# Moving seven stores behind the value loads, and the second feature pair's loads a tile forward, between two gates of a gMLP

## The chip, the cores and the metric

The kernel runs on one core of one Trainium2 chip. The metric is the device time of one execution in microseconds (us). Before the change it was 1759.82 us in the median of three runs (1759.15 to 1762.06). Executions of the same program differ by some 3 us, so a change of 2 us can hardly be read from whole times.

In the traces, PE is the matmul engine (TensorE), DVE is VectorE, ACT is ScalarE, and SP is the engine that issues all DMAs here, in one queue and in the order of the program.

## The reference, cut to what matters

The reference is an attention block followed by a gated MLP. The change sits in the second half:

```python
z  = gelu(einsum('bsd,df->bsf', h, w_in))          # h: 2048 tokens x 1024
z1 = z[..., :1792]
z2 = layernorm(z[..., 1792:], axis=-1)              # the "values"
g  = einsum('ts,bsf->btf', w_sp, z2) + b_sp[None, :, None]    # the "gate": mixes tokens
y  = einsum('bsf,fd->bsd', z1 * g, w_out)           # the "projection"
x  = x + gb * y
```

## The kernel before

The kernel makes the gate for tokens 0 to 1023 (the first gate), projects four token tiles of that half, makes the gate for tokens 1024 to 2047 (the second gate), and projects the rest. The features are cut into seven pairs of 256 (`p` = 0 to 6). One block of a gate handles one pair: it makes four output quarters with seven products of eight 128x128 by 128x512 matmuls. Some operands are sums or differences of quarters, which VectorE makes (`z_sum`). The values wait in DRAM; each pair is loaded in two loads (`k` = 0 and 1, 512 KB each, one for each half of the tokens that are summed over), and ScalarE norms them in place, eight 128x256 operations for each load.

```python
def load_z(c, p, k):                    # value load, L1408
    t = zr[c, p, k] = heap.take("zr", [P, 8, 256], FP16)
    nc.sync.dma_start(t[:], z2_dram[8 * k:8 * k + 8, :, p * 256:(p + 1) * 256]
                      .rearrange("t p f -> p t f"))

def norm_z(c, p, k, ts=range(8), by_dve=False):
    for t in ts:                        # ScalarE, L1418
        z, q = zr[c, p, k][:, t, :], 8 * k + t
        # ... (a branch for VectorE is cut)
        nc.scalar.activation(z, z, ACT.Identity, scale=z_rs[:, q:q + 1], bias=z_nm[:, q:q + 1])

def z_sum(c, p, m):                     # VectorE; m == 1 is L1429, and needs both loads' values
    a11, a21, a12, a22 = (zq(c, p, k, i) for k in range(2) for i in range(2))
    if m == 1:
        zs[c, p] = heap.take("zs", [P, 2, 8, P], FP16)
        nc.vector.tensor_add(out=zs[c, p][:, 0], in0=a21, in1=a22)
    # ... (m = 2, 3, 4 are cut)

def store_zk():                         # gated features of tokens 512..1023, kept for the end; L1617
    for p in range(NG):
        nc.sync.dma_start(zk_dram[p], z1T[0, p][:, :, 512:1024])

def project(ti, between=()):            # one token tile of the projection
    if ti + 2 < 4:
        load_x1(ti + 2)                 # residual of a later tile, L1559
    # ... 28 matmuls into bo (L1569), outt = bo + residual on VectorE (L1490),
    # ... some of VectorE's waiting tasks, then the output store (L1577)
```

The hooks of a gate block fix VectorE's order. The ones that matter:

```python
g.on(1 if p else 2, lambda: norm_z(c, p + 1, 0))
g.on(7, lambda: z_sum(c, p + 1, 1))
g.on(5, lambda: z_sum(c, p + 1, 3), lambda: z_sum(c, p + 1, 2))
g.on(5, lambda: norm_z(c, p + 2, 1))
```

And the loop that the change edits:

```python
for ti in range(4):
    if ti == 1:
        load_z(1, 0, 0)
        load_z(1, 0, 1)
        store_zk()
    elif ti == 2:
        load_b(1)                       # the bias, L1403
        load_z(1, 1, 0)
        load_z(1, 1, 1)
        load_z(1, 2, 1)
        norm_z(1, 0, 0)
        norm_z(1, 0, 1)
    project(ti, last + [weights] if not ti else ())
while tasks:
    tasks.pop(0)()
heap.give(*(z1T[0, p] for p in range(NG)))
norm_z(1, 1, 1)
```

The softmax here doesn't subtract the row's maximum and nothing guards it: scores larger than these inputs give would overflow.

## Time and profile before

| what | value | view |
|---|---|---|
| time | 1759.82 us (1759.15 to 1762.06, 3 runs) | the runs |
| span of the profiled run | 1760.4 us, granted clock 1.0 | the page |
| PE busy | 1740.1 us, 99% | the page, part 1 |
| matmul to matmul, 512 columns | 0.216 us | timeline of PE |
| PE's delays in the first 25 us of the second gate | 0.61 + 1.60 = 2.21 us | timeline of PE |
| ScalarE starts the second pair's norms | 1.83 us after the gate's first matmul | timeline of ACT |

Lines of the page, before:

```profile
span 1760.4 us, 23835 instructions
...
PE 1740.1 (99%) x8542; PEld 799.5 (45%) x8542; DVE 1502.9 (85%) x2284; ACT 1298.5 (74%) x1529; POOL 30.5 (2%) x39
...
PE 88%; DVE 6%; DMA 3%; ACT 2%; issue 1%; SPq 0%; DVEq 0%; ACTq 0%
```

PE is busy nearly all the time. The Trainium skill ("Perfetto Trace Analysis", Identifying the Most-Contended Engine) warns that matmul busy time is a bad measure of the distance to the roofline, because matmuls are pipelined. Here, too, busy time hides what matters: one matmul's record lasts 0.379 us but the next starts 0.216 us later, so a delay is seen best in the distance from start to start. 0.216 us is what the skill gives for a warm array ("TensorE: Matmul & The Clock Gate", Wait — 56ns, not 53.3ns?: 215.7 ns for 512 columns), and this trace agrees. I call *delay* what a distance has over 0.216 us.

From the timeline of PE, before: start, duration, engine, line, operation and tiles, count, and in brackets the idle time before and what ended it. The first line is the start of the second gate.

```profile
1606.66 1.03 PE L965 MATMUL a<-s_slots,zr 128*128 128x512 f16 x4
...
1617.90 1.03 PE L965 MATMUL c<-s_slots,zr 128*128 128x512 f16 x4
1619.38 1.89 PE L965 MATMUL a<-h_slots 128*128 128x512 f16 x8 [0.45 <-DVE snap L1490]
1622.70 1.02 PE L965 MATMUL a<-wq_t 128*128 128x512 f16 x4 [1.44 <-DVE snap L1490]
```

Four matmuls from 1617.90 should end their turn at 1618.77; the next starts at 1619.38. Eight from 1619.38 should end theirs at 1621.11; the next starts at 1622.70. Both times PE waited for a snapshot that VectorE takes of a PSUM bank before PE may go on accumulating in it. The reader should not stop there. The chain of waits, before (start, duration, what), leads further back:

```profile
1599.86 8.54 DMA zr<-z_dram
...
1608.49 2.12 ACT zr L1418 x5
...
1610.96 5.51 ACT zr L1418 x11
...
1616.49 0.69 DVE wq_t L1429
1617.18 1.20 DVE w_t_15636 L1390 x2
1618.39 0.33 DVE units L1612
1618.72 0.61 DVE snap L1490
...
1622.04 0.61 DVE snap L1490
...
1622.70 1.89 PE a L965 x8
```

A value load of 8.54 us from its issue to its landing, then sixteen norms, then the sum that needs them, and behind that sum, in VectorE's order, the snapshots. The timelines of ACT and DVE, before, show the idle time at both hand-overs:

```profile
1598.36 4.03 ACT L1418 ACTIVATE h_slots<-h_slots,z_nm,z_rs 128x256 f16<-128x256 f16 x8
1608.49 11.90 ACT L1418 ACTIVATE zr<-zr,z_nm,z_rs 128x256 f16<-128x256 f16 x24 [6.10 <-DMA zr<-z_dram]
...
1614.12 0.41 DVE L1612 TENSOR_TENSOR w_out<-w_out 128x512 f16<-128x512 f16 x1
1616.49 0.69 DVE L1429 TENSOR_TENSOR wq_t<-zr 128x1024 f16<-128x1024 f16 x1 [1.96 <-ACT zr L1418]
```

And the DMA queue, before, shows why the load came late: stores are issued first (and, not shown here, a residual, an output store and the bias).

```profile
1590.32 0.70 SPq L1408 DMA_DIRECT2D h_slots<-z_dram  x1
1591.06 3.71 SPq L1617 DMA_DIRECT2D zk_dram<-z1T  x4
...
1599.27 5.64 SPq L1408 DMA_DIRECT2D zr<-z_dram  x3
```

### The profile page before, as it was taken

What the parts mean: (1) busy time and instruction counts of PE and PEld (TensorE: products, weight loads), DVE (VectorE), ACT (ScalarE), POOL (GpSimd) and SP (SyncE); (2) the same over time, 40 slices, a digit from 0 to 9 for tenths busy, and PEclk for the clock granted to TensorE, in tenths of its full rate; (3) what the DMA queues carried; (4) which work ended last, traced back from release to release, by engine and by line L of the source; (5) the groups of instructions that cost most, each with busy time, mean ns of one, the idle gap of its engine ahead of it and who ended that gap; (6) DMA issues with size and microseconds to landing.
All of it is one profiled execution on the core that took longest, in us unless ns stands there. A gap on an engine that the chain in (4) does not pass through costs nothing.

```text
span 1760.4 us, 23835 instructions
## 1 busy us (share of the span) xinstructions
PE 1740.1 (99%) x8542; PEld 799.5 (45%) x8542; DVE 1502.9 (85%) x2284; ACT 1298.5 (74%) x1529; POOL 30.5 (2%) x39
## 2 busy tenths in 40 slices
PE   7999999999999999999999999999999999999999
PEld 4444444444444444444444444444444444444444
DVE  6898898898988898989999988986679788788975
ACT  6998889999999999999999999711235666736600
POOL 1000000000000000000000000000000000000000
PEclk9999999999999999999999999999999999999999
DMA  8575466646544643555653474645758544558222
GB/s 252 132 181 143 114 142 160 160 126 151 156 131 130 165 114 96 145 138 137 160 123 102 116 189 127 189 125 159 177 154 218 143 122 122 179 128 219 61 78 96
DMA packets 452999, 253.52 MB, mean 144 GB/s; under 512 B 293776, under 2 KB 412816, under 8 KB 452880
## 3 DMA queue, kind: packets, MB, share of 16 engines
q1 hardware_dynamic: 452880, 252.00, 54.2%
q8 instruction: 67, 1.10, 0.3%
q14 instruction: 52, 0.43, 0.1%
HBM read 146.02 MB, written 55.59 MB: 115 GB/s over the span
## 4 chain that ended last, share of the span: by engine, by line
PE 88%; DVE 6%; DMA 3%; ACT 2%; issue 1%; SPq 0%; DVEq 0%; ACTq 0%
PE sps L509 23%; PE ops L777 23%; PE a L965 16%; PE b L965 9%; PE c L965 4%; PE qa L490 4%; PE qps L407 4%; PE qb L490 3%; DMA wm<-in_w_mod_dram 1%; ACT pt L840 1%; PE bo L1569 1%; PE a_11218 L965 1%; PE mps L201 1%; DVE sum L1013 0%; DMA zr<-z_dram 0%
## 5 line engine op out<-in xcount | busy, mean ns | idle before, releaser
L840 ACT ACTIVATE pt<-sps 128x1024 bf16<-128x1024 f32 x1008 | 1004.6, 1024 | 80.9 <-PE sps L509 37.3
L509 PE MATMUL sps<-qT,kT 128*128 128x512 bf16 x2048 | 609.2, 379 | 2.4 <-ACT pt L840 1.2
L777 PE MATMUL ops<-pt,v_sb 128*128 128x512 bf16 x2048 | 598.9, 379 | 0.0
L509 PEld LDWEIGHTS <-kT 128*128 128x128 bf16 x2048 | 199.3, 98 | 246.5 <-issue 14.8
L777 PEld LDWEIGHTS <-v_sb 128*128 128x128 bf16 x2048 | 200.1, 98 | 243.2 <-issue 1.6
L1008 ACT ACTIVATE snap<-a 128x512 f32<-128x512 f32 (+1 forms) x111 | 60.7, 565 | 115.4 <-PE a L965 105.0
L965 PEld LDWEIGHTS <-h_slots 128*128 128x128 f16 (+1 forms) x716 | 70.0, 98 | 84.1 <-issue 1.6
L856 DVE COPY ou<-ops 128x512 f32<-128x512 f32 x126 | 81.1, 686 | 30.0 <-PE ops L777 27.4
L407 PE MATMUL qps<-h1T,wq_t 128*128 128x512 bf16 x288 | 96.7, 379 | 0.0
L1013 DVE TENSOR_TENSOR sum<-b,snap 128x512 f32<-128x512 f32 (+1 forms) x76 | 50.0, 658 | 46.9 <-PE b L965 28.0
L1418 ACT ACTIVATE zr<-zr,z_nm,z_rs 128x256 f16<-128x256 f16 x90 | 45.0, 586 | 47.9 <-DMA zr<-z_dram 40.9
L665 DVE TENSOR_TENSOR oT<-ou,rbc 128x1024 bf16<-128x1024 f32 x62 | 75.3, 1214 | 1.4 <-DMA rbc<-rec_dram 1.4
L475 DVE COPY tx<-qa 128x512 f32<-128x512 f32 x66 | 45.4, 688 | 31.3 <-PE qa L490 31.3
L643 DVE TENSOR_REDUCE den<-pT 128x8 f32<-128x1024 bf16 x58 | 68.7, 1185 | 0.7 <-DMA pT<-sums_dram 0.7
L965 PEld LDWEIGHTS <-s_slots 128*128 128x128 f16 (+1 forms) x415 | 40.3, 98 | 50.5 <-DVE s_slots L1338 1.5
L490 PE MATMUL qa<-h1s,wq_t 128*128 128x512 f16 x176 | 63.0, 379 | 0.0
L490 PEld LDWEIGHTS <-wq_t 128*128 128x128 bf16 (+1 forms) x352 | 34.4, 98 | 41.6
L965 PEld LDWEIGHTS <-wq_t 128*128 128x128 f16 (+1 forms) x344 | 33.6, 98 | 40.8 <-DVE wq_t L1431 1.0
L148 POOL TENSOR_TENSOR rstd<-var,neg_half 128x1 f32<-128x1 f32 x30 | 25.0, 835 | 1303.1 <-DVE var L146 1275.4
L470 DVE TENSOR_TENSOR qT<-qb,tx 128x512 bf16<-128x512 f32 x66 | 45.2, 684 | 0.7
L407 PEld LDWEIGHTS <-wq_t 128*128 128x128 bf16 x288 | 28.2, 98 | 33.9 <-issue 0.6
L490 PEld LDWEIGHTS <-tx 128*128 128x128 f16 x264 | 25.8, 98 | 31.2
(962 smaller groups left out, 2575.0 us busy)
## 6 DMA issues: line engine op xcount, KB each, us to landing
rbc<-rec_dram SPq DMA_DIRECT2D x63, 512.0 KB
v_sb<-in_A_v_cache_dram SPq DMA_DIRECT2D x40, 512.0 KB
oT_dram<-oT SPq DMA_DIRECT2D x62, 256.0 KB
sums_dram<-pacc SPq DMA_DIRECT2D x58, 256.0 KB
wm<-in_w_mod_dram SPq DMA_DIRECT2D x12, 1024.0 KB
wq_t<-in_A_wq_dram SPq DMA_DIRECT2D x7, 1024.0 KB
zr<-z_dram SPq DMA_DIRECT2D x12, 512.0 KB
h_slots<-oT_dram SPq DMA_DIRECT2D x10, 512.0 KB
```

The source lines that it names most:

```text
L407: nc.tensor.matmul(box["ps"][:], weights[:, dc, hc:hc + DH], src[:, dc, q0:q0 + 512], start=(n == 0), stop=(n == KD - 1))
L475: nc.vector.tensor_copy(out=x if m == 6 else su, in_=a)
L490: nc.tensor.matmul(box["b" if m in (2, 7, 4) else "a"][:], *operand(m, dc), start=(m in (1, 2, 7) and dc == 0), stop=(dc == 3), skip_group ...
L509: nc.tensor.matmul(sps[:, j * 512:(j + 1) * 512], kts[h][:, kb * P:(kb + 1) * P], qts[(h, qh)][:, j * 512:(j + 1) * 512], start=True, stop ...
L643: nc.vector.tensor_reduce(out=den[:], in_=state[i]["pT"][:], op=ALU.add, axis=mybir.AxisListType.X)
L665: nc.vector.tensor_mul(out=oT, in0=state[i]["ou"][:], in1=state[i]["rbc"][:])
L777: nc.tensor.matmul(o_ps[j][:], vs[halves[i][0]][:, kb, :], pt_tiles[g][:, j * 512:(j + 1) * 512], start=(kb == 0), stop=(kb == NKB - 1))
L840: nc.scalar.activation(pt_tiles[g], s_tiles.pop(g)[:], ACT.Exp, scale=SCALE, **bias)
L856: nc.vector.tensor_copy(out=ou[:, j * 512:(j + 1) * 512], in_=o_ps[j][:])
L965: nc.tensor.matmul(self.ps[self.BANK[n]], a, b, start=(n in (1, 2, 7) and k == 0), stop=(k == len(lhs) - 1), skip_group_check=True)
L1008: nc.scalar.activation(t, ps, ACT.Copy)
L1013: nc.vector.tensor_add(out=t, in0=ps, in1=snap)
```

## The change

The seven stores are not needed until the end of the kernel; the second pair's values are needed within 10 us. The change moves the stores behind the value loads and loads the second pair right behind the first pair, one projection tile sooner. It also writes the norms sooner in the program and swaps the two loads of each pair, so that the one normed first is loaded first.

```diff
     for ti in range(4):
         if ti == 1:
-            load_z(1, 0, 0)
-            load_z(1, 0, 1)
+            for k in ((0, 1), (0, 0), (1, 1), (1, 0)):
+                load_z(1, *k)
+        elif ti == 2:
+            norm_z(1, 0, 1)
+            norm_z(1, 0, 0)
+            load_b(1)
             store_zk()
-        elif ti == 2:
-            load_b(1)
-            load_z(1, 1, 0)
-            load_z(1, 1, 1)
             load_z(1, 2, 1)
-            norm_z(1, 0, 0)
-            norm_z(1, 0, 1)
+        elif ti == 3:
+            norm_z(1, 1, 1)
         project(ti, last + [weights] if not ti else ())
     while tasks:
         tasks.pop(0)()
     heap.give(*(z1T[0, p] for p in range(NG)))
-    norm_z(1, 1, 1)
```

## The prediction

> **What bounds the kernel now.** TensorE. The page gives PE 1740.1 us busy of a 1760.4 us span (99%), granted clock 1.0, and the chain that ended last is 88% PE. The change touches the stage between first and second gate: the four projection tiles of the first half (1585 to 1607 us) and the first two blocks of the second gate (1607 to 1625 us). In PE's timeline, 512-column matmuls follow each other every 0.216 us there; from 1480 us to the end only three places are later: 0.61 us before 1619.38, 1.60 us before 1622.70, 0.29 us before 1691.8. So at most 2.2 us, 0.13% of the span, is to be had.
>
> **Where those 2.2 us come from.** The waits put both on VectorE's snapshots (L1490). The chain of waits goes further back: snapshot <- value sum (L1429) <- ScalarE norms (L1418) <- a value load. In the DMA queue, the second pair's loads are issued at 1599.3 and 1599.9 us, after seven stores of gated features (1591.1 to 1597.2), a residual load, an output store and the bias; by their semaphores they land at 1606.6 and 1608.4. ScalarE, idle for 6.1 us, starts norming at 1608.49; two tiles of 8 x 0.5 us end at 1616.49; VectorE sits idle 1.96 us before the sum that needs them. The Trainium skill ("DMA: Bandwidth & Descriptors", Issuing engines are not separate DMA queues) says all DMAs run on the same 16 engines and interleave; in this trace landings follow the order of issue, about 0.65 us per 256 KB store and 1.6 us per 512 KB load.
>
> **What the change does.** No arithmetic and no bytes are added or removed; some buffers change. The second pair's loads move from behind the stores to right behind the first pair's: issued at about 1591 and 1592, landed at about 1597.7 and 1599.4. ScalarE then norms four tiles without a break, 1594.4 to about 1610.5, six us sooner. The stores go out about 1596.5 to 1602.5 and land by about 1609; VectorE's first unit, which rewrites a stored buffer, comes at 1612: 3 us to spare. The buffers that the early loads take were last read by PE before 1585.1 us, so they should not block the queue. The third pair's load lands about 1 us later, before ScalarE wants it.
>
> **How much is critical.** VectorE's idle 1.96 us goes. Its order stays, so I step its durations on from 1614.46: sum 0.61, two weight sums 1.21, unit 0.33, snapshot to 1617.3 (PE wants it at 1618.8: first gap gone), then gate, product, two value sums, unit, snapshot to about 1620.6, against PE's 1620.5. The second gap shrinks to 0.1-0.3 us. Gain 2.0 us. Thereafter VectorE is as far behind PE as now, without a stall: nothing is given back. Predicted 1757.8 us, range 1756.2 to 1759.6; the spread of runs (1759.15 to 1762.06) is as large as the gain. Faster by over 2%: 0.005; within 2%: 0.99; slower: 0.005.
>
> **What would show it.** Right: value loads landed by 1600; ScalarE's 6.1 us idle and VectorE's wait for the norms gone; PE's two gaps together under 0.4 us; all later work 2 us earlier, the gap near 1690 unchanged. Wrong: units or later value loads wait for the late stores (a new gap at 1612 to 1640); the early loads delay the residual load of tile 3 or the queue blocks on the output store; or they slow the first pair so that the first gate product starts late.

## The result

After: 1759.23 us in the median of four runs (1757.53 to 1760.77); before, in the same rounds and with the earlier runs, 1760.17 us (1759.15 to 1762.06). The ratio is 0.9993 with a 95% interval of 0.9976 to 1.001: no change within 2%, and nothing that these runs can tell from noise.

Lines of the page, after:

```profile
span 1755.8 us, 23842 instructions
...
PE 1737.0 (99%) x8542; PEld 797.9 (45%) x8542; DVE 1502.9 (86%) x2284; ACT 1298.6 (74%) x1529; POOL 30.5 (2%) x39
...
PE 92%; DVE 5%; DMA 1%; ACT 1%; issue 1%; SPq 0%; DVEq 0%; ACTq 0%
```

The profiled spans differ by 4.6 us, but not all of that is the change. The second gate's first matmul starts at 1606.66 us before and at 1604.08 us after, but the projection's first matmul is already 2.58 us sooner (1576.45 against 1579.03 us), and PE had no delay in the projection of either run: these 2.58 us lie ahead of anything that the change could touch. The rest, 2.04 us, lies in the stage. From the timeline of PE, after:

```profile
1604.08 1.03 PE L965 MATMUL a<-s_slots,h_slots 128*128 128x512 f16 x4
...
1615.32 1.03 PE L965 MATMUL c<-s_slots,zr 128*128 128x512 f16 x4
1616.18 1.89 PE L965 MATMUL a<-h_slots,zr 128*128 128x512 f16 x8
1618.07 1.02 PE L965 MATMUL a<-wq_t 128*128 128x512 f16 x4
```

The first delay is gone (1615.32 to 1616.18 is four matmuls' time), and of the second 0.165 us is left (1616.18 to 1618.07, where eight matmuls take 1.73). The timelines of ACT and DVE, after:

```profile
1591.60 4.04 ACT L1418 ACTIVATE zr<-zr,z_nm,z_rs 128x256 f16<-128x256 f16 x8 [30.42 <-DMA zr<-z_dram]
1595.54 4.02 ACT L1418 ACTIVATE h_slots<-h_slots,z_nm,z_rs 128x256 f16<-128x256 f16 x8
1599.47 11.89 ACT L1418 ACTIVATE zr<-zr,z_nm,z_rs 128x256 f16<-128x256 f16 x24
...
1611.54 0.41 DVE L1612 TENSOR_TENSOR w_out<-w_out 128x512 f16<-128x512 f16 x1
1611.88 0.68 DVE L1429 TENSOR_TENSOR wq_t<-zr 128x1024 f16<-128x1024 f16 x1
```

ScalarE's 6.10 us of idle time and VectorE's 1.96 us are gone. The DMA queue, after, has all four loads ahead of the stores:

```profile
1588.49 2.85 SPq L1408 DMA_DIRECT2D zr<-z_dram  x2
...
1594.42 2.66 SPq L1617 DMA_DIRECT2D zk_dram<-z1T  x4
```

To compare the two runs, I give landings in us from the second gate's first matmul. They are the last of each DMA's sixteen semaphore increments in the trace.

```
                        before    after
first pair, loads   -12.33 -10.63   -12.57 -10.43
second pair, loads   -0.02  +1.74    -8.62  -6.88
seven stores         -9.95..-5.71    -4.14..-0.12
tile 3's residual       -5.08    -6.09
bias                    -1.92    -4.82
third pair, load        +3.38    +1.54
```

### The profile page after: what moved, and what is told of

The parts are those of the page before. It is cut to its first block, busy times and chain, and to the rows that moved or that the text cites. A ratio compares the mean times of both kernels' runs of the same rounds, so it can differ in the third digit from the quotient of the medians.

```text
span 1755.8 us, 23842 instructions
## 1 busy us (share of the span) xinstructions
PE 1737.0 (99%) x8542; PEld 797.9 (45%) x8542; DVE 1502.9 (86%) x2284; ACT 1298.6 (74%) x1529; POOL 30.5 (2%) x39
## 4 chain that ended last, share of the span: by engine, by line
PE 92%; DVE 5%; DMA 1%; ACT 1%; issue 1%; SPq 0%; DVEq 0%; ACTq 0%
PE sps L509 24%; PE ops L777 24%; PE a L965 16%; PE b L965 9%; PE c L965 4%; PE qa L490 4%; PE qps L407 4%; PE qb L490 3%; PE bo L1569 1%; ACT pt L840 1%; DMA wm<-in_w_mod_dram 1%; PE a_11218 L965 1%; PE mps L201 1%; DVE sum L1013 0%; DVE stats L154 0%
```

## The experiments

Eleven more runs were made (e1 is the changed kernel again), all with correct results; all profiled runs had a granted clock of 0.998 to 1.0. Runs with a profile alone: I compare only stage times, never their whole times. For each I read the same numbers, in us: when the second pair's last norm ends and when its sum starts on VectorE, both from the second gate's first matmul; PE's delays within 25 us of that matmul (one of 0.02 us that nearly all profiles have is left out); and the *stage time*, from the second gate's first matmul to the end of the kernel's last one.

| kernel | norms end | sum starts | PE's delays | stage time |
|---|---|---|---|---|
| before | +9.80 | +9.83 | 2.21 | 150.76 |
| after | +3.35 | +7.80 | 0.17 | 148.72 |
| after again (e1) | +3.73 | +7.80 | 0.17 | 148.73 |
| order of norms and first pair alone (e6) | +9.44 | +9.47 | 1.85 | 150.41 |
| two loads swapped alone (e3) | +8.17 | +8.20 | 0.59 | 149.15 |
| stores moved alone (e2) | +6.06 | +7.80 | 0.17 | 148.73 |
| loads moved alone (e4) | +3.26 | +8.26 | 0.65 | 149.19 |
| loads moved, residual ahead (e11) | +4.07 | +7.80 | 0.17 | 148.73 |
| loads later still (e5) | +11.20 | +11.23 | 3.60 | 152.17 |
| after, stores last (e9) | +3.52 | +7.80 | 0.17 | 148.72 |
| after, one VectorE move (e7) | +3.54 | +7.80 | 0.00 | 148.57 |
| after, two VectorE moves (e8) | +3.47 | +7.80 | 0.00 | 148.44 |
| e8, products 3 and 4 swapped (e10) | +3.54 | +7.80 | 0.00 | 148.40 |

Before was profiled only once. But in every profile the stage time less all of PE's delays (the one near the end of the gate included, 0.29 us in most) is 148.25 to 148.29 us, although e1 to e11 ran on three different chips. So, to within 0.04 us, the stages differ by PE's delays and by nothing else.

My theory is that only one time counts, the end of the second pair's norms; VectorE reaches the sum at +7.80 by itself, and every microsecond that the norms end later is a microsecond of PE. The rivals are that the stores must leave the way because they compete for the DMA engines, that the sooner place in the program counts, and that part of the gain is given back later.

### e1: the changed kernel again, five rounds

No edit.

> The changed kernel again, five rounds. Theory (only PE's two gaps in the first blocks of the second gate go): mean 2 us under before, ratio about 0.9988; the profile shows 0.17 us left of the 2.21 us of gaps there. Rival (the medians, 0.94 us apart, are right and half of the gain is given back somewhere): ratio about 0.9995, and a new gap after 1640 us. Either ratio may be within the noise; the gaps decide.

Measured: 1758.70 us in the median (1757.19 to 1759.24), against 1760.77 us (1758.31 to 1761.85, nine runs) of before on the same chip; ratio 0.9989, interval 0.9976 to 1.0001. The profile shows 0.17 us of delay in the stage and the old 0.29 us near the end of the gate, nothing new. The mean lies where the theory has it, but the interval just includes no change; the stage time, 148.73 against 148.72 us, is what repeats. Nothing is given back.

### e6: the program's order alone

```diff
         if ti == 1:
-            load_z(1, 0, 0)
             load_z(1, 0, 1)
+            load_z(1, 0, 0)
             store_zk()
         elif ti == 2:
+            norm_z(1, 0, 1)
+            norm_z(1, 0, 0)
             load_b(1)
             load_z(1, 1, 0)
             load_z(1, 1, 1)
             load_z(1, 2, 1)
-            norm_z(1, 0, 0)
-            norm_z(1, 0, 1)
+        elif ti == 3:
+            norm_z(1, 1, 1)
```

(and the `norm_z(1, 1, 1)` behind the loop taken away)

> Before, with only the order in the program changed as the change has it: the first pair's two loads swapped, its norms written ahead of the bias and the loads, the second pair's first norm written a projection tile sooner. Loads of the second pair and stores stay. Theory: ScalarE has nothing else to do there and waits for data, so nothing moves: gaps 2.2 us. Rival (norming sooner in the program helps): gaps under 1.5 us.

Measured: 1.85 us of delay, so most of it stays, as the theory had it, but not exactly 2.21. The 0.36 us of difference is the same 0.36 us by which the norms ended sooner (9.44 against 9.80): the second pair's later load happened to land that much sooner against PE in this run (+1.39 against +1.74). ScalarE was idle until its data came, wherever the norms stood in the program. This part of the change does nothing for the time by itself.

### e3: the second pair's two loads swapped, nothing else

```diff
             load_b(1)
-            load_z(1, 1, 0)
             load_z(1, 1, 1)
+            load_z(1, 1, 0)
             load_z(1, 2, 1)
```

> Before, with only the two loads of the second pair's values swapped, so that the tile that ScalarE norms first is loaded first; all seven stores stay ahead of both. Theory (what counts is when ScalarE can start on the third tile): that tile lands at 1606.6 instead of 1608.4, ScalarE starts 1.8 us sooner, its second tile ends at about 1614.7 against VectorE's 1614.46, so PE's two gaps shrink from 2.21 to about 0.4 us. Rival (the stores have to leave the way of the loads, as the change has it): the gaps stay over 1.9 us.

Measured: 0.59 us of delay in place of 2.21, with all seven stores still ahead of the loads. (I expected about 0.4, from a start 1.8 us sooner; ScalarE started 1.64 us sooner against PE, +0.19 for +1.83.) From the timelines of ACT, DVE and PE of this run:

```profile
1606.77 11.91 ACT L1418 ACTIVATE zr<-zr,z_nm,z_rs 128x256 f16<-128x256 f16 x24 [4.61 <-PE bo L1569]
...
1614.78 0.69 DVE L1429 TENSOR_TENSOR wq_t<-zr 128x1024 f16<-128x1024 f16 x1 [0.32 <-ACT zr L1418]
...
1621.00 1.02 PE L965 MATMUL a<-wq_t 128*128 128x512 f16 x4 [0.42 <-DVE snap L1490]
```

In before, the load that ScalarE wanted first was issued second, so ScalarE waited for both. Swapping them lets it start when the first lands (1606.69 us; the bracket names a matmul, which ended just by then, but the landing 0.08 us before the start fits better), and the second lands during the first's norms. Two lines of source give 1.61 of the 2.04 us (150.76 less 149.15). The rival, by which over 1.9 us stay until the stores leave the way, is out; the other 0.42 us need loads that land sooner still, as in e2. Timed over five rounds: 1758.60 us (1757.14 to 1760.49), ratio 0.9991, interval 0.9978 to 1.0003; again not to be told from no change.

### e2: the stores moved, nothing else

```diff
             load_z(1, 0, 1)
-            store_zk()
         elif ti == 2:
             load_b(1)
             load_z(1, 1, 0)
             load_z(1, 1, 1)
+            store_zk()
             load_z(1, 2, 1)
```

> Before, with only the seven stores moved behind the two loads of the second pair (which stay a tile later than in after, behind tile 1's output store and the bias). Theory: the loads land by about 1603, just as ScalarE ends the first pair, so the gaps shrink to the same 0.17 us as in after; loading a tile sooner was not needed. Rival (the earlier issue is what helps): gaps of 1 us or more are left.

Measured: 0.17 us of delay and 148.73 us of stage time, all of the gain. From the timelines of ACT, DVE and PE of this run:

```profile
1604.73 11.91 ACT L1418 ACTIVATE zr<-zr,z_nm,z_rs 128x256 f16<-128x256 f16 x24 [2.61 <-PE bo L1569]
...
1614.44 0.68 DVE L1429 TENSOR_TENSOR wq_t<-zr 128x1024 f16<-128x1024 f16 x1
...
1618.75 1.89 PE L965 MATMUL a<-h_slots 128*128 128x512 f16 x8
1620.65 1.02 PE L965 MATMUL a<-wq_t 128*128 128x512 f16 x4
```

(The bracket again names a matmul that ended just by then; the load landed 0.08 us before the start.) The loads landed at 1602.96 and 1604.65 us, later than expected (the bias ahead of them took until 1601.18), and the norms ended at +6.06, still 1.7 us ahead of VectorE. Loading the second pair a tile sooner was not needed: moving the stores, or nearly so the swap, is enough.

### e4 and e11: the loads moved, the stores left where they were

```diff
             load_z(1, 0, 1)
+            load_z(1, 1, 0)
+            load_z(1, 1, 1)
             store_zk()
         elif ti == 2:
             load_b(1)
-            load_z(1, 1, 0)
-            load_z(1, 1, 1)
             load_z(1, 2, 1)
```

> Before, with only the second pair's loads moved up behind the first pair's, ahead of the stores; the stores, the norms and the order within a pair stay as they were. Theory: gaps as in after, 0.17 us. Rival (the reordered norms do part of the work): more than 0.5 us is left.

Measured: a miss. The norms ended at +3.26, as in after, and the old delay nearly went (0.045 us), but a new one of 0.61 us came, in the first block. From the timelines of DVE and PE of this run:

```profile
1604.50 0.69 DVE L1490 SCALAR_TENSOR_TENSOR outt<-bo,x1r 128x512 bf16<-128x512 f32 x1 [1.73 <-DMA x1r<-x_dram]
...
1610.17 1.02 PE L965 MATMUL a<-wq_t,zs 128*128 128x512 f16 x4 [0.44 <-DVE snap L1490]
```

VectorE waited 1.73 us for the residual of projection tile 3, which had queued behind four loads and seven stores and landed at 1604.40 us. PE did not feel that at once; VectorE then carried the lag into the gate and was late with the first block's snapshot. The rival's number (more than 0.5 us) fits too, so this run alone does not decide between the residual and the norms, which stand here as in before. To test it, e11 adds one edit: the residual of tile 3 is loaded ahead of the four value loads.

```diff
         if ti == 1:
+            load_x1(3)
             load_z(1, 0, 0)
 ...
     def project(ti, between=()):
-        if ti + 2 < 4:
+        if ti + 2 < 3:
             load_x1(ti + 2)
```

> The run with only the loads moved up (stores ahead of tile 3's residual) with one more edit: tile 3's residual is loaded ahead of the value loads. Theory (its new gap of 0.61 us came from VectorE's 1.73 us wait for that residual, which had queued behind loads and stores): the wait goes, and so does that gap; 0.17 us or less is left in the first blocks, and 0.29 us near 1690. Rival (the gap is DMA contention or the unswapped first pair): 0.6 us stays.

Measured: VectorE's wait for the residual is gone, and so is the new delay; 0.17 us is left and the stage takes 148.73 us, the same as after. The same two instructions as above, from the timelines of DVE and PE of this run:

```profile
1600.35 0.69 DVE L1490 SCALAR_TENSOR_TENSOR outt<-bo,x1r 128x512 bf16<-128x512 f32 x1 [0.53 <-PE bo L1569]
...
1606.64 1.02 PE L965 MATMUL a<-wq_t,zs 128*128 128x512 f16 x4
```

The norms and the first pair stand as in before, so a new order of the norms is not needed for this. So with the loads moved up, something has to keep the residual from waiting behind loads and stores together. In the change it is the stores' new place, behind the residual.

### e5: the loads later still

```diff
             load_b(1)
+            load_z(1, 2, 1)
             load_z(1, 1, 0)
             load_z(1, 1, 1)
-            load_z(1, 2, 1)
```

> Before, with the second pair's loads issued one load later still (behind the third pair's). Theory: the tile that ScalarE wants first lands 1.6 us later, at about 1610, and every microsecond of it reaches PE: gaps of about 3.8 us in place of 2.2 (slope 1). Rival (PE's gaps come from VectorE's order, the load is only near in time): they stay at 2.2 us.

Measured: 3.60 us of delay; the norms ended at +11.20 in place of +9.80. From the timelines of DVE and PE of this run, and from its waits (who waited for what, us in total, times, longest):

```profile
1616.93 0.69 DVE L1429 TENSOR_TENSOR wq_t<-zr 128x1024 f16<-128x1024 f16 x1 [3.35 <-ACT zr L1418]
...
1619.82 1.89 PE L965 MATMUL a<-h_slots 128*128 128x512 f16 x8 [0.75 <-DVE snap L1490]
1623.14 1.02 PE L965 MATMUL a<-wq_t 128*128 128x512 f16 x4 [1.44 <-DVE snap L1490]
...
PEld L965 <- ACT zr L1418: 1.9, 5, 0.4
```

The norms ended 1.40 us later than in before and PE's delays grew by 1.39 us. Four points, e5, before, e6 and e3, lie on one line, delays = (end of the norms) - 7.59: 3.61, 2.21, 1.85 and 0.58 against 3.60, 2.21, 1.85 and 0.59 measured. In the five runs in which the norms end before +7.80, the residual is in time and VectorE's order is untouched (after, e1, e2, e9, e11), the delays stay at 0.17. So the delays follow the norms' end with slope 1 (measured from +8.17 to +11.20), down to a floor; after the change the norms have 4.45 us to spare (7.80 less 3.35). The way is not the same in all four, though. In before the whole 2.21 us is lost at the snapshots; in e5 only 2.51 of the 3.60 us is. The other 1.09 us is four steps of 0.49 us between matmuls, from 1615.00 to 1616.96, in which PE's weight loads (PEld) waited for ScalarE's norms themselves. The sum behind the last norm still came last, and so set the total.

### e9: the stores later still

```diff
             load_b(1)
-            store_zk()
             load_z(1, 2, 1)
 ...
         project(ti, last + [weights] if not ti else ())
+    store_zk()
     while tasks:
         tasks.pop(0)()
```

> After, with the seven stores moved later still, behind the output store of projection tile 3 (about 11 us later in the queue). The prediction gave the stores 3 us to spare, because VectorE's first unit was said to rewrite a stored buffer. Rival that I now hold: the program's own waits show that this unit rewrites no stored buffer; the later value loads do, and their users come over 10 us later. It expects the later value loads to land about 4.6 us later than in after, ScalarE to idle some 4 us, and PE's gaps to stay at 0.17 and 0.29 us. The prediction's reading expects VectorE to wait some 2 us or more at the first unit, and a new PE gap there.

Measured: delays unchanged, 0.17 and 0.29 us, stage time 148.72 us. The stores landed from 1608.93 to 1614.13 us. From the timelines of DVE and ACT of this run:

```profile
1610.43 0.42 DVE L1612 TENSOR_TENSOR units<-w_out 128x512 f16<-128x512 f16 x1
...
1617.72 4.04 ACT L1418 ACTIVATE h_slots<-h_slots,z_nm,z_rs 128x256 f16<-128x256 f16 x8 [5.16 <-DMA h_slots<-z_dram]
```

VectorE's first unit, at 1610.43, waited for no store, although five of the seven had not landed. From the first store's issue (1606.41) up to this unit, VectorE waited on a DMA's semaphore only once, at 1606.64, and no store used that one before 1609.09. The third pair's other load landed at 1617.63 us and ScalarE idled 5.16 us for it; nothing reached PE. The 3 us of slack that the prediction gave the stores were in the wrong place: by the program's waits the rewriters of the stored buffers are later value loads, and their users come later still. The trace fits this: right before SP issues the value load of 1614.65, it waits on the semaphores that the third and the seventh store use.

### e7, e8 and e10: what is left of the delays

In after, VectorE makes a weight difference of 0.34 us ahead of the snapshot that PE waits for. e7 moves that one behind the snapshot:

```diff
         for n, k in ((2, 3), (6, 1), (7, 2), (5, 4)):
-            g.on(n, lambda p=p, k=k: wp_sum(p, k))
+            (gates[1][1] if (p, n) == (0, 5) else g).on(
+                1 if (p, n) == (0, 5) else n, lambda p=p, k=k: wp_sum(p, k))
```

> After, with only the first of the two VectorE moves: one weight difference of the first block behind the snapshot. Theory: the 0.17 us gap goes, the 0.29 us gap near 1687 us stays. Rival: no change, or the lag comes back as a gap in the next block.

Measured: the 0.17 us delay is gone, the 0.29 us one stays, no new one; stage time 148.57 us. e8 adds the same for a feature difference of the sixth block:

```diff
-        for n, k in ((1, 2), (2, 3), (3, 4)):
+        for n, k in ((1 + (p == NG - 2), 2), (2, 3), (3, 4)):
             g.on(end, lambda p=p, n=n, k=k: after(n, lambda: p_sum(1, p, k)))
```

> After, with two small VectorE instructions moved behind a snapshot that PE waits for: one weight difference (0.34 us) of the first block of the second gate, one feature difference (0.34 us) of its sixth. Theory (the 0.17 us and 0.29 us that are left are VectorE's order): both PE gaps go to 0.05 us or less, so PE has no gap from 1480 us to the end, 0.45 us less than after. Rival (they are PE or semaphore latency): both stay.

Measured: the first delay is gone, but of the second 0.16 us is left, where I expected 0.05 or less. (A delay of 0.73 us at 1480.2 us is not new: before has it at 1479.66, just outside the window that I had read.) The timelines of DVE and PE of this run:

```profile
1688.56 0.69 DVE L1490 SCALAR_TENSOR_TENSOR snap<-a,b_bc 128x512 f32<-128x512 f32 x1 [0.24 <-PE a L965]
1689.28 0.69 DVE L1490 SCALAR_TENSOR_TENSOR g<-b,snap 128x512 f16<-128x512 f32 x1
...
1690.03 1.02 PE L965 MATMUL b<-s_slots,zr 128*128 128x512 f16 x4
```

VectorE now waits for PE, so its order is no longer the cause; two dependent operations stand between two products, with only 1.51 us of other matmuls to cover them. The Trainium skill ("Perfetto Trace Analysis", Optimizing Scalar/DVE Operations) says that where ScalarE or VectorE are not saturated but cause bubbles on other engines, breaking up their instructions may help; no run here tried that, and reordering them was enough for the first delay. Timed over five rounds: 1758.73 us (1757.19 to 1760.35), ratio 0.9988, interval 0.9974 to 1.0002.

e10 lets product 3, which needs the snapshot alone, go ahead of product 4:

```diff
     f.run(1)
-    prev.run(4)
     prev.run(3)
+    prev.run(4)
```

(and the buffers and feature differences that hung on product 3 of the last block now hang on product 4)

> After with both VectorE moves, and the last gate's products 3 and 4 swapped: product 3 needs the snapshot only, product 4 also the operation behind it (1.47 us from the end of product 5 to the start of product 4, against 1.51 us of product 1 in between). Theory: the last 0.16 us gap goes; but the next product needs what product 4 feeds, about 1.2 us after its end against 1.3 us until its seventh operand, so it is close: 0.1 us may come back there. Rival (a fixed latency of switching): 0.16 us stays. The time is under 0.5 us from after either way and will not be resolved.

Measured: the 0.16 us delay went, and 0.11 us came back at the seventh operand of the next product, as feared. Stage time 148.40 us, the shortest of all: 0.32 us under after and 2.36 us under before. Timed over three rounds: 1757.68 us (1757.47 to 1758.44, four runs) against 1760.86 us (1760.0 to 1762.25, seven runs) of before; ratio 0.9983, interval 0.9966 to 1.0. By the stage time e10 beats both kernels; the whole times can't tell it from after.

## Why the prediction was right

- **The bound and the place.** Right: only PE's 2.21 us of delay in the first two blocks of the second gate were to be had by this change (the 0.29 us near the end, of which e8 and e10 took 0.18, are another matter), and e5, before, e6 and e3 show that they follow the end of the second pair's norms, microsecond for microsecond.
- **The size.** 2.0 us predicted, 2.04 us measured in the stage (150.76 to 148.72), and again in e1 (148.73). The first delay went, as said; the second shrank to 0.165 us, within the 0.1 to 0.3 us said. VectorE's durations, stepped on by hand from the timeline, were enough for this.
- **The time.** 1757.8 us predicted; measured 1759.23, inside the range of 1756.2 to 1759.6 but near its end. Two of the four runs took 1760.4 us or more. e1 gave 1758.70. The difference to 1757.8 is not explained by the stage, which gave all that was said; it is within what executions differ by. That the median fell inside the range, 0.37 us from its end, is thus in part luck; the stage time is not.
- **The landings.** With the run's own shift of 2.58 us added, the second pair landed at 1598.0 and 1599.8 us (said: 1597.7 and 1599.4), and the four tiles were normed from 1594.2 to about 1610.0 (said: 1594.4 to 1610.5). The 1.6 us for a 512 KB load was a little low: the two of the second pair and the third pair's took 1.90, 1.76 and 1.63 us in before.
- **Nothing given back.** Right: the delay near the end of the gate was 0.287 us before and 0.289 after.
- **Wrong in a step that did not matter: the third pair's load.** It was said to land 1 us later; it landed 1.84 us sooner against PE (+1.54 in place of +3.38). The bias, a broadcast load, landed 2.48 us after the DMA ahead of it before, and 0.60 us after. That difference of 1.88 us fits; why the prediction had the load 1 us later, with the same DMAs ahead of it as before, the record does not show. The stores landed sooner too, by 1606.5 with the shift (said: 1609).
- **Wrong in a step that did not matter: the slack of the stores.** "VectorE's first unit, which rewrites a stored buffer" was a guess about the allocator. e9 shows that this unit waits for no store.
- **Not seen: which part does the work.** The text took moving the loads a tile sooner as the working part. e2 shows that moving the stores alone gives all of it, e3 that swapping two loads gives 1.61 us of it, and e4 that moving the loads alone gives less than the whole, because then tile 3's residual is late. That last risk was named in the prediction; what kept it away was the stores' new place.

## What to carry to other kernels

A wait that PE shows on VectorE may start three engines back: follow the chain to the first one that was idle for want of data, and ask what stood ahead of that data in its queue. In a queue that works in order, first issue what is wanted first, and check what the moved transfers now stand ahead of (here a residual). When the gain is 0.1% of the time, read it as the time of a stage that starts behind the noise; here it repeats to 0.01 us, while whole times of one program differ by 3 us.

## What the Trainium skill lacked or had wrong

- "DMA: Bandwidth & Descriptors" (Queues, rings and completion order) says that on each DMA engine descriptors are consumed in ring order but that completion is not first in, first out; its example is a DMA on one engine behind a DMA on sixteen. Nothing here contradicts that: each of these DMAs made sixteen increments. But in all thirteen profiles, the 30 to 32 DMAs issued from SP between 1576 and 1640 us reached their last semaphore increment in the order of issue, so a wanted load did wait for everything issued ahead of it. For DMAs issued from SP, what that costs is told only as bandwidth; here, among those that landed over 4.6 us after their issue, landings came 0.66 us after the one ahead for a 256 KB store (median of 77; 0.43 to 0.99) and 1.79 us for a 512 KB value load in 512-byte pieces (median of 114; 1.60 to 3.50).
- The same page gives no duration for a load that broadcasts one row to 128 partitions. The bias (256 KB written) landed from 0.60 us (after) to 3.49 us (e2) after the DMA ahead of it. It goes by kernel: 0.60 to 0.72 us in the six profiles with the change's early loads and late stores, 1.41 and 1.43 in e11 and e4, 2.32 to 2.89 in before, e3, e5 and e6. What decides this stays open.
- "Perfetto Trace Analysis" has nothing on how much executions of one program differ. Here the second gate's first matmul came between 1603.17 us (e11) and 1607.18 us (e8) in thirteen profiles, at granted clocks of 0.998 to 1.0, although PE had no delay in the projection ahead of it, while the stage behind it repeated to 0.01 us.
